# The last token group of two feed-forward layers: products of 128 rows cut into two of 64 rows, summed apart and joined by VectorE

## The chip, the cores and the metric

The kernel runs on one core of a Trainium2 chip. The metric is the device time of one execution in microseconds (us). The engines are called as the profile calls them: PE is TensorE's matmul, PEld its load of stationary operands, DVE is VectorE, ACT is ScalarE, POOL is GpSimd and SP is SyncE, which issues the DMAs here. A *product* is one matmul instruction with the load that belongs to it.

## The reference

A windowed attention gives 1536 tokens of 512 values; two feed-forward layers of 512 -> 2048 -> 512 follow. The changed code is the end of the second one.

```python
def _moe2_ref(x, w_in, w_out) -> np.ndarray:
    h = x @ w_in
    relu6 = np.clip(h + 3.0, 0.0, 6.0)
    g = h * relu6 / 6.0
    return (g @ w_out).astype(np.float32)

def reference(**kwargs):
    ...
    attn_out = _attn_ref(**attn_kwargs)
    B, H, S, D = attn_out.shape
    x = np.ascontiguousarray(attn_out.transpose(0, 2, 1, 3)).reshape(B * S, H * D)
    x = _moe_ref(x=x, **moe_kwargs)
    return _moe2_ref(x=x, **moe2_kwargs)
```

## The kernel before

The 1536 tokens are three groups of 512 (`GB`), and the 2048 hidden values sixteen chunks of 128 (`NCH`), whose weights pass through the core in phases of 6, 5 and 5 chunks per layer (`PHASES`). Each operand of the layers stands as a high and a low float32r part (`xsh` and `xsl`, `gh` and `gl`, two weight tiles each), and each mathematical product is three products on the chip: low by high, high by low, high by high, in that order of all three over the list it is given (`matmul3`, L209; its instruction is L214, which all layer products share in the profile).

`item` (L277) does one chunk for one group: twelve products of 128 rows by 512 columns make `h` in one PSUM bank (four parts of the 512 inputs, `KC`, by three), ACT and DVE make `gh` and `gl` from it (`split_g`, L184: ACT's relu at L203, DVE's product at L204, ACT's cast to `gh` at L205, DVE's subtraction to `gl` at L206), and twelve more products add to four sums `acc`, one per 128 tokens. In the second layer `gh` and `gl` are the stationary operand of those.

The last group of the last phase is `last_items` (L323). It makes the five `h` (named `hz`) and their `g` first, calls `check_step` between them (which at its end puts one small transposition `pf`, L666, on PE), and then takes the 128 tokens `m` one after the other: fifteen products into one sum `accz`, the three of a chunk together, one DVE instruction that adds a sixth of it to `part` (L355), one DMA of the result. The last 128 tokens go as two halves of 256 columns, to end on a short piece. PSUM banks rotate: `h_bank` (L98) goes round four banks by its count `n_h`, `acc_tags` names the four banks of the sums.

The order of the instructions on each engine is not that of the code alone: the context is opened with `schedule_with_timeline_sim=True` (L871), so a planner with costs of its own sets it, and PE, ACT and DVE each work through their own list in that order. Products of the group before (`acc`) therefore stand between those of the last one.

Of the kernel before, what the change touches and what calls it, by code (L numbers as in the profile page):

```python
# [7 lines left out]
F32 = mybir.dt.float32  # L8
# [4 lines left out]
ALU = mybir.AluOpType  # L13
# [3 lines left out]
P = 128  # L17
# [4 lines left out]
KC = DM // P  # L22
# [4 lines left out]
GT, GB = 256, 512  # L27
# [27 lines left out]
class Layers:  # L55
# [153 lines left out]
    def matmul3(self, out, pairs, start, stop, **kw):  # L209
# [3 lines left out]
        def one(z, a, b):  # L213
            return self.nc.tensor.matmul(  # L214
                out, lhsT=a, rhs=b, start=start and z == 0, stop=stop and z == len(seq) - 1, **kw
            )

        return [lambda z=z, ab=ab: one(z, *ab) for z, ab in enumerate(seq)]

    def first_items(self):  # L220


        n = PHASES[0][0] // 2
        runs = [(g, 0, EARLY_PAIRS) for g in range(EARLY)] + [(EARLY, 0, n)]
        runs += [(g, EARLY_PAIRS, n) for g in range(EARLY)] + [(g, 0, n) for g in range(EARLY + 1, T // GT)]
        return [(g, s, s == a, s == b - 1, a > 0) for g, a, b in runs for s in range(a, b)]
# [96 lines left out]
    def last_items(self, ph, G, spare_step):  # L323


        nc, part = self.nc, self.part[G]
        if self.hint:
            self.tc.mark_branch_hint_location("redo", engines=list(mybir.ALL_ENGINES))
        g, W = [], []
        for s in range(PHASES[1][ph]):  # L330
            W.append(self.W[NCH + sum(PHASES[1][:ph]) + s])
            wih, wil = (t.rearrange("p (k c) -> p k c", k=KC) for t in W[s][0:2])
            h = self.h_bank(f"hz{s}")
            for call in self.matmul3(
                h, [((wih[:, c], wil[:, c]), (self.xsh[G][:, c, :], self.xsl[G][:, c, :])) for c in range(KC)], True, True
            ):
                call()
            wp, t = self.free.pop(0)
            where = [wp.tile([P, CW], F32R, tag=f"w{i}_{t}", name=f"g{i}_{s}") for i in range(2)]
            g.append(self.split_g(1, h, f"z{s}", where))  # L340
            for _ in range(4):
                spare_step()
        for m in range(4):
            acc = self.bank(self.acc_tags[m], f"accz{m}")
            t0 = G * GB + m * P
            ms = slice(m * P, (m + 1) * P)
            for cs in (slice(0, 512),) if m < 3 else (slice(0, 256), slice(256, 512)):
                if cs.start:
                    acc = self.h_bank("accz4")
                for s, (gh, gl) in enumerate(g):  # L350
                    pair = ((gh[:, ms], gl[:, ms]), (W[s][2][:, cs], W[s][3][:, cs]))
                    for call in self.matmul3(acc[:, cs], [pair], s == 0, s == len(g) - 1, skip_group_check=True):
                        call()
                pm = part[:, m, cs]
                nc.vector.scalar_tensor_tensor(  # L355
                    out=pm, in0=acc[:, cs], scalar=1.0 / 6.0, in1=pm, op0=ALU.mult, op1=ALU.add
                )
                nc.sync.dma_start(out=self.out[t0:t0 + P, cs], in_=pm)
# [516 lines left out]
```

## Time and profile before

| | us |
|---|---|
| median of three runs | 630.69 (630.36 to 631.89) |
| the profiled execution, whole | 630.09 |
| its span, first to last instruction | 628.3 |
| PE busy in the span | 613.8 (98%) |
| DVE, ACT, POOL busy | 448.8, 375.3, 132.0 |
| first product of the last group (`hz`) | at 591.44 |
| last DVE instruction of the span's results | at 624.60, 0.42 long |

A busy PE says only that some product is in it: the record of a product is longer than the distance to the next one, since products overlap at their ends. What a product costs is read from start to start, and where a line of the timeline merges several, from the merged duration less that of one record. Times in the timeline count from the start of the span.

### The profile page before, as it was taken

The numbers are of one execution on the slowest core, as the hardware profiler recorded it, in microseconds if no ns is written. First come the engines' busy times: TensorE is split into PE (matmuls) and PEld (weight loads), VectorE is DVE, ScalarE is ACT, GpSimd is POOL, SyncE is SP. The second block draws the span as 40 slices with busy tenths as digits, with TensorE's granted clock in tenths as the row PEclk, the third lists the DMA queues.
The fourth block names the chain that finished last, engine by engine and source line by source line (L and its number), as shares of the span: only waits on it lengthen the run. The fifth ranks groups of instructions, "written<-read, shape, count | busy, mean of one in ns | idle before, by whom it ended". The sixth has DMA issues, their size and how long they took to land.

```text
span 628.3 us, 9717 instructions
## 1 busy us (share of the span) xinstructions
PE 613.8 (98%) x3495; PEld 514.8 (82%) x3496; DVE 448.8 (71%) x945; ACT 375.3 (60%) x796; POOL 132.0 (21%) x168
## 2 busy tenths in 40 slices
PE   8898999999999999999999999999999999999997
PEld 4587878899999888877788888888888888888886
DVE  7995687635799999999998996224999633424262
ACT  6986888774778887776788852425455742222130
POOL 3474353430132233533301410000100000000000
PEclk9998999999999999999999999999999999999999
DMA  8763312101144343333401143001457620001011
GB/s 278 272 196 106 106 39 69 35 14 68 68 133 137 96 139 119 123 107 117 140 34 57 45 135 101 1 1 33 142 191 233 207 67 1 1 0 68 1 67 69
DMA packets 26804, 59.91 MB, mean 95 GB/s; under 512 B 2688, under 2 KB 9344, under 8 KB 26752
## 3 DMA queue, kind: packets, MB, share of 16 engines
q1 hardware_dynamic: 26752, 59.26, 28.8%
q8 instruction: 28, 0.46, 0.3%
q14 instruction: 24, 0.20, 0.1%
HBM read 56.10 MB, written 3.15 MB: 94 GB/s over the span
## 4 chain that ended last, share of the span: by engine, by line
PE 74%; DVE 18%; ACT 4%; issue 2%; POOL 1%; DMA 0%; SPq 0%; POOLq 0%; ACTq 0%; DVEq 0%
PE acc L214 25%; PE h L214 24%; PE accf L214 8%; PE hf L214 6%; ACT pm L548 3%; PE ptp L571 2%; DVE wa L146 2%; PE accz L214 2%; PE hz L214 2%; PE px L589 2%; DVE wa L147 2%; DVE w L152 2%; PE s L537 2%; DVE t L200 1%; DVE t L199 1%
## 5 line engine op out<-in xcount | busy, mean ns | idle before, releaser
L214 PE MATMUL h<-xsh,w 128*128 128x512 f32 x584 | 154.7, 390 | 0.4 <-DVE t L200 0.4
L214 PEld LDWEIGHTS h<-xsh,w 128*128 128x128 f32 x584 | 109.1, 188 | 24.1 <-DVE t L200 1.8
L140 POOL TENSOR_SCALAR wa<-wa 128x512 f32<-128x512 f32 x52 | 67.4, 1300 | 242.7 <-ACT wa L137 242.7
L214 PE MATMUL acc<-w,gh 128*128 128x512 f32 x344 | 105.9, 389 | 0.0
L214 PE MATMUL h<-xsl,w 128*128 128x512 f32 x292 | 80.8, 389 | 0.0
L206 DVE TENSOR_TENSOR gl<-t,gh 128x512 fp32r<-128x512 f32 x73 | 51.3, 703 | 40.5 <-ACT gh L205 40.4
L214 PE MATMUL acc<-gh,w 128*128 128x512 f32 x240 | 77.7, 391 | 1.2 <-ACT gh L205 1.0
L214 PEld LDWEIGHTS acc<-w,gh 128*128 128x128 f32 x344 | 64.6, 188 | 13.5
L203 ACT ACTIVATE t<-h,three 128x512 f32<-128x512 f32 x43 | 29.5, 687 | 75.2 <-PE h L214 75.0
L204 DVE SCALAR_TENSOR_TENSOR t<-t,h 128x512 f32<-128x512 f32 x43 | 29.4, 684 | 61.4 <-ACT t L203 61.3
L432 POOL TENSOR_SCALAR pm<-pm,rs 128x256 f32<-128x256 f32 (+1 forms) x96 | 56.6, 607 | 67.5 <-DVE rs L430 31.8
L205 ACT CAST gh<-t 128x512 fp32r<-128x512 f32 x73 | 45.2, 619 | 41.4 <-PE acc L214 23.3
L214 PE MATMUL acc<-w,gl 128*128 128x512 f32 x172 | 66.9, 389 | 0.0
L214 PEld LDWEIGHTS h<-xsl,w 128*128 128x128 f32 x292 | 54.7, 188 | 11.4
L214 PE MATMUL accf<-ghf,w 128*128 128x256 f32 x288 | 58.7, 293 | 0.5 <-ACT ghf L205 0.5
L214 PEld LDWEIGHTS acc<-gh,w 128*128 128x128 f32 x240 | 44.8, 188 | 11.6 <-ACT gh L205 1.9
L548 ACT ACTIVATE pm<-pm,nm 128x256 f32<-128x256 f32 (+1 forms) x96 | 46.2, 483 | 5.6 <-DVE nm L543 5.3
L214 PEld LDWEIGHTS accf<-ghf,w 128*128 128x128 f32 x288 | 47.8, 196 | 0.9 <-ACT ghf L205 0.8
L214 PE MATMUL hf<-xsh,w 128*128 128x256 f32 x288 | 47.1, 289 | 0.0
L214 PE MATMUL acc<-gl,w 128*128 128x512 f32 x120 | 46.7, 389 | 0.0
L151 ACT CAST w<-wa 128x512 fp32r<-128x512 f32 x56 | 34.4, 615 | 17.3 <-DVE wa L147 9.6
L214 PE MATMUL accf<-glf,w 128*128 128x256 f32 x144 | 41.5, 288 | 1.5 <-DVE glf L206 1.5
(122 smaller groups left out, 1060.1 us busy)
## 6 DMA issues: line engine op xcount, KB each, us to landing
raw<-in_w2i SPq DMA_DIRECT2D x16, 512.0 KB, 3.3
raw<-in_w2o SPq DMA_DIRECT2D x16, 512.0 KB, 3.3
raw<-in_w1i SPq DMA_DIRECT2D x14, 512.0 KB, 3.8
raw<-in_w1o SPq DMA_DIRECT2D x12, 512.0 KB, 3.3
V<-in_v SPq DMA_DIRECT2D x12, 256.0 KB, 3.3
range<-in_w1i SPq DMA_DIRECT2D x6, 512.0 KB, 3.7
range<-in_w1o SPq DMA_DIRECT2D x6, 512.0 KB, 4.4
chk<-in_q SPq DMA_DIRECT2D x12, 256.0 KB, 2.7
```

The costliest lines, as they stand in the source:

```text
L140: nc.gpsimd.tensor_scalar(out=a, in0=a, scalar1=W_HI, scalar2=W_LO, op0=ALU.min, op1=ALU.max)
L146: nc.vector.scalar_tensor_tensor(out=ai, in0=hi, scalar=-2 ** 30, in1=ai, op0=ALU.bitwise_and, op1=ALU.bitwise_or)
L147: nc.vector.scalar_tensor_tensor(out=ai, in0=lo, scalar=29, in1=ai, op0=ALU.logical_shift_right, op1=ALU.bitwise_or)
L151: nc.scalar.copy(wh, a)
L152: nc.vector.tensor_tensor(out=wl, in0=a, in1=r32(wh), op=ALU.subtract)
L203: nc.scalar.activation(t1, hf, AF.Relu, bias=self.three[:, 0:1])
L204: nc.vector.scalar_tensor_tensor(out=t3, in0=t1, scalar=6.0, in1=hf, op0=ALU.min, op1=ALU.mult)
L205: nc.scalar.copy(gh, t3)
L206: nc.vector.tensor_tensor(out=gl, in0=t3, in1=r32(gh), op=ALU.subtract)
L214: return self.nc.tensor.matmul(out, lhsT=a, rhs=b, start=start and z == 0, stop=stop and z == len(seq) - 1, **kw)
L432: nc.gpsimd.tensor_scalar(out=t, in0=t, scalar1=rs[:, j:j + 1], scalar2=0.0, op0=ALU.mult, op1=ALU.add)
L548: nc.scalar.activation(pmz, pmz, AF.Exp, bias=nm[:, z:z + 1], scale=-1.0, accum_out=sm[:, z:z + 1])
```

## The change

`last_items` alone is changed. Each product of 128 rows in it, but for those of the last 128 tokens, becomes two of 64 rows, rows 0 to 63 and rows 64 to 127 of both operands, which lie in the upper and the lower half of the array. Each half has a sum of its own in a bank of its own (`matmul3_rows`). For `h`, ACT copies the first sum to an SBUF tile `hsz` and DVE adds the second to it there, and `split_g` works on that tile. For the tokens, DVE adds both sums to `part`, one after the other, so that a pair of banks serves `m` = 0 and 2, the other `m` = 1. Two things come with it: the fifteen products of a sum are now ordered low by high over all five chunks first, then high by low, then high by high; and the planner makes a new order of the whole group.

```diff
+    def matmul3_rows(self, outs, pairs):
+
+        seq = [(a[x], b[y]) for x, y in ((1, 0), (0, 1), (0, 0)) for a, b in pairs]
+        for z, (a, b) in enumerate(seq):
+            for r, out in enumerate(outs):
+                rows = slice(r * P // 2, (r + 1) * P // 2)
+                self.nc.tensor.matmul(out, lhsT=a[rows], rhs=b[rows], start=z == 0, stop=z == len(seq) - 1)
...
-            h = self.h_bank(f"hz{s}")
-            for call in self.matmul3(
-                h, [((wih[:, c], wil[:, c]), (self.xsh[G][:, c, :], self.xsl[G][:, c, :])) for c in range(KC)], True, True
-            ):
-                call()
+            hs = [self.h_bank(f"hz{s}_{r}") for r in range(2)]
+            self.matmul3_rows(
+                hs, [((wih[:, c], wil[:, c]), (self.xsh[G][:, c, :], self.xsl[G][:, c, :])) for c in range(KC)]
+            )
+            h = self.tp.tile([P, 512], F32, tag="t", name=f"hsz{s}")
+            nc.scalar.copy(h, hs[0])
+            nc.vector.tensor_tensor(out=h, in0=hs[1], in1=h, op=ALU.add)
...
-        for m in range(4):
-            acc = self.bank(self.acc_tags[m], f"accz{m}")
+        for m in range(3):
+            accs = [self.bank(self.acc_tags[2 * (m % 2) + r], f"accz{m}_{r}") for r in range(2)]
+            ms = slice(m * P, (m + 1) * P)
+            self.matmul3_rows(accs, [((gh[:, ms], gl[:, ms]), W[s][2:4]) for s, (gh, gl) in enumerate(g)])
+            pm = part[:, m, :]
+            for acc in accs:
+                nc.vector.scalar_tensor_tensor(
+                    out=pm, in0=acc, scalar=1.0 / 6.0, in1=pm, op0=ALU.mult, op1=ALU.add
+                )
+            t0 = G * GB + m * P
+            nc.sync.dma_start(out=self.out[t0:t0 + P, :], in_=pm)
+        for m in (3,):
+            acc = self.bank(self.acc_tags[2], f"accz{m}")
...
-            for cs in (slice(0, 512),) if m < 3 else (slice(0, 256), slice(256, 512)):
+            for cs in (slice(0, 256), slice(256, 512)):
```

Up to the first `hz` all engines have the same list as before. From there on the order differs. Three places of it follow; `hz_0`, `accz_0` are sums of the upper half, `hz_1`, `accz_1` of the lower, and L226 (after) is the new product line, L214 that of whole products in both.

The first is PE's list at the start of the group, where the `acc` products of the group before come in between. Before:

```order
L214 MATMUL hz_92_6161<-xsh_77,w_27_4878 128x512 x4
L214 MATMUL hz_92_6161<-xsl_80,w_27_4877 128x512 x4
L214 MATMUL hz_92_6161<-xsh_77,w_27_4877 128x512
L214 MATMUL acc_5985<-w_30_5157,gl_6090 128x512
L214 MATMUL acc_5985<-w_30_5158,gh_6089 128x512
```

After:

```order
L226 MATMUL hz_1_93_6162<-xsh_77,w_27_4878 128x512
L226 MATMUL hz_0_92_6161<-xsh_77,w_27_4878 128x512
L226 MATMUL hz_1_93_6162<-xsh_77,w_27_4878 128x512
L226 MATMUL hz_0_92_6161<-xsl_80,w_27_4877 128x512
L214 MATMUL acc_5985<-w_30_5157,gl_6090 128x512
L214 MATMUL acc_5985<-w_30_5158,gh_6089 128x512
```

Half products stand in turn, upper and lower, and whole products follow them directly; here they cut in after an upper one whose lower one comes twelve whole products later.

The second is PE's list at the fourth and fifth chunk. Before:

```order
L666 MATMUL pf_6264<-ident,m_6257 1x128
L214 MATMUL hz_96_6275<-xsh_77,w_30_5156 128x512 x4
L214 MATMUL hz_96_6275<-xsl_80,w_30_5155 128x512 x4
L214 MATMUL hz_96_6275<-xsh_77,w_30_5155 128x512 x4
L214 MATMUL accz_6317<-w_27_4879,g_0_6175 128x512
L214 MATMUL hz_97_6296<-xsh_77,w_31_5258 128x512 x4
```

After:

```order
L226 MATMUL hz_0_99_6323<-xsh_77,w_30_5155 128x512 x4
L226 MATMUL accz_0_6397<-w_27_4879,g_0_6191 128x512
L226 MATMUL accz_1_6398<-w_27_4879,g_0_6191 128x512
L226 MATMUL accz_0_6397<-w_28_4969,g_1_6240 128x512
L226 MATMUL accz_1_6398<-w_28_4969,g_1_6240 128x512
L226 MATMUL accz_0_6432<-w_27_4879,g_0_6191 128x512
L226 MATMUL accz_1_6433<-w_27_4879,g_0_6191 128x512
L226 MATMUL accz_0_6432<-w_28_4969,g_1_6240 128x512
L226 MATMUL accz_1_6433<-w_28_4969,g_1_6240 128x512
L226 MATMUL hz_1_100_6324<-xsh_77,w_30_5156 128x512 x4
L226 MATMUL hz_1_100_6324<-xsl_80,w_30_5155 128x512 x4
L226 MATMUL hz_1_100_6324<-xsh_77,w_30_5155 128x512 x4
```

The fourth chunk's twelve upper products (the last four are the first row) all stand ahead of its twelve lower ones, with four pairs of `accz` between.

The third is where the last chunk's `g` is first used (`g_4`; of the two tiles with that name, the one with the higher last number is `gl`). PE before:

```order
L214 MATMUL accz_6353<-w_30_5157,g_3_6289 128x512
L214 MATMUL accz_6317<-w_31_5259,g_4_6310 128x512
L214 MATMUL accz_6317<-w_31_5260,g_4_6309 128x512
L214 MATMUL accz_6317<-w_31_5259,g_4_6310 128x512
L214 MATMUL accz_6335<-w_31_5259,g_4_6310 128x512
```

PE after:

```order
L226 MATMUL accz_0_6397<-w_30_5157,g_3_6353 128x512
L226 MATMUL accz_1_6398<-w_30_5157,g_3_6353 128x512
L226 MATMUL accz_0_6432<-w_30_5157,g_3_6353 128x512
L226 MATMUL accz_1_6433<-w_30_5157,g_3_6353 128x512
L214 MATMUL accz_103_6520<-w_30_5157,g_3_6353 128x256
L214 MATMUL accz_103_6520<-w_30_5158,g_3_6352 128x256
L214 MATMUL accz_103_6520<-w_30_5157,g_3_6352 128x256
L226 MATMUL accz_0_6397<-w_31_5259,g_4_6390 128x512
L226 MATMUL accz_1_6398<-w_31_5259,g_4_6390 128x512
L226 MATMUL accz_0_6397<-w_27_4880,g_0_6190 128x512
```

DVE's list that makes those `g`, before:

```order
L204 SCALAR_TENSOR_TENSOR t3z_6291<-t1z_6290,hz_96_6275 128x512
L206 TENSOR_TENSOR g_3_6289<-t3z_6291,g_3_6288 128x512
L204 SCALAR_TENSOR_TENSOR t3z_6312<-t1z_6311,hz_97_6296 128x512
L206 TENSOR_TENSOR g_4_6310<-t3z_6312,g_4_6309 128x512
L355 SCALAR_TENSOR_TENSOR part_92<-accz_6317,part_92 128x512
```

DVE after:

```order
L347 TENSOR_TENSOR hsz_6349<-hz_1_100_6324,hsz_6349 128x512
L204 SCALAR_TENSOR_TENSOR t3z_6355<-t1z_6354,hsz_6349 128x512
L206 TENSOR_TENSOR g_3_6353<-t3z_6355,g_3_6352 128x512
L347 TENSOR_TENSOR hsz_6386<-hz_1_102_6361,hsz_6386 128x512
L204 SCALAR_TENSOR_TENSOR t3z_6392<-t1z_6391,hsz_6386 128x512
L206 TENSOR_TENSOR g_4_6390<-t3z_6392,g_4_6389 128x512
```

Before, 33 whole products stand on PE between the last `hz` and the first use of `g_4`; after, eight half products and twelve whole ones of 256 columns do. On DVE one instruction more stands in each chunk's chain, behind the subtraction of the chunk before.

## Rows read from the trace of the kernel before

**Rows 1.** The page: span, busy time, granted clock in 40 slices (tenths).

```profile
span 628.3 us, 9717 instructions
PE 613.8 (98%) x3495; PEld 514.8 (82%) x3496; DVE 448.8 (71%) x945; ACT 375.3 (60%) x796; POOL 132.0 (21%) x168
...
PEclk9998999999999999999999999999999999999999
```

**Rows 2.** The chain that ended last: start us, us, what, instructions.

```profile
611.00 13.58 PE accz L214 x74
```

**Rows 3.** Timeline, PE and PEld, last group: start us, us, instructions merged.

```profile
591.44 1.07 PE L214 MATMUL hz<-xsh,w 128*128 128x512 f32 x4
...
608.11 1.07 PE L214 MATMUL hz<-xsh,w 128*128 128x512 f32 x4
608.80 0.87 PEld L214 LDWEIGHTS hz<-xsl,w 128*128 128x128 f32 x4
609.02 1.07 PE L214 MATMUL hz<-xsl,w 128*128 128x512 f32 x4
...
610.83 13.72 PE L214 MATMUL accz<-w,g 128*128 128x512 f32 x74
```

**Rows 4.** Timeline of PE, warm-up products of bf16, whole array.

```profile
10.22 0.81 PE L683 MATMUL warm<-zeros 128*128 128x512 bf16 x3
```

**Rows 5.** Timeline of PE in the attention, one pair of half products each.

```profile
121.23 0.29 PE L214 MATMUL accf<-ghf,w 128*128 128x256 f32 x1
121.44 0.49 PE L537 MATMUL s<-kT,qT 64*128 64x256 f32 x2
121.77 0.38 PE L537 MATMUL s<-kT,qT 64*128 64x256 f32 x2
121.98 0.38 PE L537 MATMUL s<-kT,qT 64*128 64x256 f32 x2
122.20 0.38 PE L537 MATMUL s<-kT,qT 64*128 64x256 f32 x2
```

**Rows 6.** Timeline of PE, from halves (of columns) back to whole products.

```profile
143.93 0.50 PE L589 MATMUL px<-pT,V 128*64 128x128 f32 x6
144.15 0.28 PE L589 MATMUL px<-pT,V 128*64 128x128 f32 x2
144.36 0.74 PE L214 MATMUL hf<-xsh,w 128*128 128x256 f32 x4
144.93 0.64 PE L214 MATMUL hf<-xsl,w 128*128 128x256 f32 x4
```

**Rows 7.** Timeline of ACT and DVE, the last chunk's `g`.

```profile
611.09 0.69 ACT L203 ACTIVATE t1z<-hz,three 128x512 f32<-128x512 f32 x1 [0.88 <-PE hz L214]
611.81 0.69 DVE L204 SCALAR_TENSOR_TENSOR t3z<-t1z,hz 128x512 f32<-128x512 f32 x1 [0.88 <-ACT t1z L203]
612.54 0.62 ACT L205 CAST g<-t3z 128x512 fp32r<-128x512 f32 x1 [0.76 <-DVE t3z L204]
613.19 0.69 DVE L206 TENSOR_TENSOR g<-t3z,g 128x512 fp32r<-128x512 f32 x1 [0.69 <-ACT g L205]
```

**Rows 8.** Timeline, the end of the span.

```profile
624.60 0.42 DVE L355 SCALAR_TENSOR_TENSOR part<-accz,part 128x256 f32<-128x256 f32 x1 [1.37 <-PE accz L214]
```

**Rows 9.** PE's two longest waits near the start, in brackets.

```profile
22.30 0.44 PE L589 MATMUL px<-pT,V 128*64 128x128 f32 x4 [1.05 <-ACT pT L573]
...
51.18 0.38 PE L214 MATMUL accf<-glf,w 128*128 128x256 f32 x1 [1.46 <-DVE glf L206]
```

**Rows 10.** Stretches: length, PE, PEld, DVE, ACT, POOL busy, granted clock, DMA.

```profile
51.00:52.00 1.00, 0.82 (x5) 0.82 (x6) 1.00 (x3) 1.00 (x5) 0.00 (x0) 0.75 0.80 188
52.00:53.00 1.00, 1.00 (x6) 1.00 (x6) 1.00 (x4) 0.97 (x4) 0.00 (x0) 0.50 0.24 90
...
54.00:55.00 1.00, 1.00 (x7) 1.00 (x6) 0.69 (x1) 0.25 (x1) 1.00 (x2) 0.55 0.00 0
...
591.00:625.00 34.00, 33.56 (x163) 28.13 (x161) 14.44 (x25) 7.86 (x12) 0.00 (x0) 1.00 0.16 59
```

## The prediction, made before the changed kernel ran

> **What bounds the kernel now.** I read the page first: PE is busy in 613.8 of 628.3 us [rows 1], so the kernel is as long as its products. Then the chain that ended last, whose last long piece is the `accz` products [rows 2]: what is lost or won on PE in the last group moves the end. Then the timeline of that group. It starts at 591.44, PE never waits in it, and the 74 `accz` products go through in one piece from 610.83 [rows 3]. The granted clock is 1.00 (2.4 GHz) from 591 to 625 [rows 10].
>
> The pitch from product to product is what the change is about. Four products start at 608.11 and the next four at 609.02 [rows 3]: 0.91 / 4 = 0.227 us for 512 columns of float32r. Products of 256 columns stand 0.12 apart (four in 0.64, less one record of 0.29, by three [rows 5, 6]). 512 columns in bf16, over the whole array too, take (0.81 - 0.38) / 2 = 0.215, with 0.38 for one record [rows 4]. So a float32r product pays about 0.012 more than that, whether it is long or short. That is all that halving can win.
>
> **What half products cost, by the attention.** There the trace has products in two halves of 64 rows. Each line "x2" at L537 is one pair, one for each half, and both lie inside one record's length, so the halves do run side by side. Pairs start at 121.77, 121.98 and 122.20: 0.215 a pair [rows 5]. They are float32, not float32r: whether a float32r pair goes at 0.215 or 0.227 the trace doesn't show. From below I bound it by 0.215 (the pair's row), from above by 0.227 + 0.012 = 0.239 (both halves pay the extra one after the other). I take **0.227**: rows 3 and 4 differ in the type alone and not in the geometry, and each half still has as many float32r products to swap in as the whole array had.
>
> The attention also shows what a change of geometry costs. From whole to halves: the last whole product starts at 121.23, the first pair at 121.44, 0.21 where 0.12 would be the pitch; and the first pair takes 0.32 to the second where 0.215 is the pitch [rows 5]. That is 0.09 + 0.11 = 0.20. Back from halves (here of columns): the pitch of pairs is (0.50 - 0.28) / 2 = 0.11, the last pair starts at 144.15 and the first whole product at 144.36, 0.10 too much; its four take 0.57 to 144.93 where 4 x 0.12 is usual [rows 6]. Again 0.19. I take **0.20 a switch**.
>
> The Trainium skill has a rule against this change ("TensorEngine Tiling (Array Packing)", Key Properties): a change of tiling mode drains TensorE. The rows agree on the drain, the first 0.09 of each switch, but show a second part of the same size after it that the rule doesn't name. By the rule alone the twelve switches below would cost 1.1 instead of 2.4 us.
>
> **The path, part by part.** Nothing changes before 591.44, since the lists are the same up to there. I call the time in which the array takes one half product, or one in each half, a slot.
>
> *Slots.* Before, the changed work is 60 `hz` and 45 `accz` products: 105 times 0.227. Afterwards it is 210 half products; paired throughout they would be 105 slots again. But PE works its list in order. Counted through the new order: the first three chunks' 72 need 37 slots, since one pair is torn by twelve `acc` products. The next 60 (fourth and fifth chunk and twelve `accz`) need 42, not 30, since twelve upper ones in a row and then twelve lower ones can't run side by side. The next 4 need 2, the last 74 need 37. Together 118, **13 more: 13 x 0.227 = 2.95 us**. The 24 `acc` products and the 30 of 256 columns stay as they are.
>
> *Switches.* The list goes from whole to half products and back twelve times: at the start, around two blocks of `acc` (four), around `pf` (two), and five from the 256-column products: **12 x 0.20 = 2.4 us**. Before there is none.
>
> *A wait for the last `g`.* The new ACT copy and DVE add lengthen the chain from `h` to `gl`. Before, ACT starts 0.48 after the last `hz` product started (610.61 by the pitch, 611.09), and relu, product, cast and subtraction end 2.79 after that, at 613.88 [rows 7]; 33 whole products cover it. In the new list I reach the last `hz` product at 591.44 + 76 slots (17.2) + 24 `acc` (5.45) + 7 switches (1.4) = 615.5. The same way, the fourth chunk's last product starts 12 slots earlier, at 612.8; its add (0.69, bounded by the L204 row, which also reads a sum and an SBUF tile [rows 7]) runs from 613.3 to 614.0, and its subtraction ends at 616.8. The fifth chunk's copy ends at 616.5 and its add would be ready for DVE then, but stands behind that subtraction in DVE's list. So it ends at 617.5, and `gl` is there at 617.55 + 2.79 = 620.35. PE arrives earlier: from 615.5, three slots (0.68), a switch, nine products of 256 columns (1.08), a switch, two slots (0.45), a switch, three products (0.36), a switch: 618.9. It **waits 1.45 us**, everything of PE is queued behind it, and as `gl` is the stationary operand, its load is exposed once more, 0.1 by the first pair of rows 5.
>
> Other additions cost nothing: ACT and DVE are busy 7.9 and 14.4 of the 34 us from 591 to 625 [rows 10], so the copies and adds of the first chunks lie under the next chunks' products; the sums' banks come free before they are needed (`m` = 2 starts 11 slots, 2.5 us, after `m` = 0 ended, against two DVE instructions of 0.69). If that cover failed, each would cost its 0.7.
>
> *The tail.* The last DVE instruction of 256 columns takes 0.42 [rows 8]. The last two sums now end 0.36 apart, so the last one waits for the first: 0.42 + 0.03 - 0.36 = 0.09.
>
> **Sum:** 2.95 + 2.4 + 1.45 + 0.1 + 0.09 = 7.0, less 0.1 for the switch to `pf`, whose single column needs no load: **+6.9 us**. On the profiled execution's own 630.09 that is 637.0; that execution lies 0.6 under the median of the runs, 630.69, so the forecast is **637.6 us**. A nanosecond more or less on a slot is worth 0.10 us: 64 slots lie ahead of the fourth chunk's last product, which sets the chain to the wait, and 37 behind the wait.
>
> **Rivals.**
>
> 1. The swap is hidden: a pair takes 0.215. For it: the pair rows, and the bf16 row. Against: both are other types. The sum falls by 101 x 0.012 = 1.2: **636.4**. The Trainium skill ("TensorE: Matmul & The Clock Gate", Part 3) says that a load overlaps a running matmul only when their row groups differ, from which halving would gain. This trace doesn't bear that out for whole products: four loads, 0.87 us from 608.80, lie under the products from 608.11 [rows 3], and a load of 0.19 fits in a pitch of 0.227 only so. I give it the chance that rows 4 and 5 give.
>
> 2. Both halves pay their swap in turn, 0.239 a pair, 1.2 more: **638.8**. Nothing in the trace shows it.
>
> 3. The clock falls at the wait. After the 1.46 us wait at 51.18 [rows 9] the granted clock was 0.50 (1.2 GHz) until about 54.9 [rows 10], though PE was at work again; a wait of 1.05 at 22.3 [rows 9] left it at 0.9 or more in its slice, the second, where the fourth, with 51.18 in it, shows 8 [rows 1]. Mine is 1.45, between the two and nearer to the one that fell; but PE is busy right up to it. Price: 3.4 us at half speed, 1.7 us: **639.3**.
>
> 4. The change doesn't do what it says: float32r halves don't run side by side. Then 210 half products take 210 x 0.227, 92 slots more, 20.9 us, less 1.2 as the wait all but goes: **657**. Against it are the pairs of rows 5, two banks, two halves, as here.
>
> 5. The other side, not slower: a half product takes less than a whole one. The place is the slot. The point from which it decides: 0.227 - 6.9 / 101 = 0.159 for no loss at all, 0.177 for less than 0.3% (1.9 us, about what a measurement of this kernel can tell from no change). At 0.159 it is **631**. For it: only that the pair's record, 0.38, is a little shorter than the whole one's 0.39. Against: the pairs' pitch of 0.215, which is the pitch of 512 columns in bf16 too.
>
> **How the numbers follow.** Forecast 40%, rival 1 24%, rival 2 10%, rival 3 12%, rival 4 9%, rival 5 5%. Switches at the drain alone (0.1) with rival 1 give 635.4, the wait being longer by half of what they save; rival 2 and the clock together give 640.5. The range 635.4 to 640.6 holds the first four cases, 86%, and leaves out 4 and 5. All but rival 5 are slower by over 0.3%, 95%; of its 5%, 3 lie within 0.3% and 2 below.
>
> **What the profile of the changed kernel would show.** Pairs of L226 0.227 apart, upper and lower a few ns from each other: slot and concurrency right; at 0.215 rival 1, single ones at 0.227 throughout rival 4. First pairs after a whole product late by 0.09 and long by 0.11: the switch. Twelve upper `hz` of the fourth chunk in series over 2.7 us: the 13 slots. PE idle 1.2 to 1.7 us at about 619 to 620.4, released by DVE's L206: the wait; a granted clock under 1.00 after it is rival 3. The forecast is wrong above all if the switch of this type costs other than the float32 rows say, twelve times, or if the copy and add are slow enough to move the wait.

## The result, and the profile after

The changed kernel takes 638.89 us (median of 4 runs, 638.02 to 639.66) against 630.87 for the kernel before (4 runs, 630.36 to 631.89): a ratio of 1.0125, 95% interval 1.0106 to 1.0143. That is 8.0 us slower. In a second comparison, described below, it took 638.35 against 631.17, 7.2 us slower (1.011, 1.007 to 1.015). The forecast was 6.9 slower, 637.6 us.

The page of the first profiled execution, which took 639.66 us, answers [rows 1]:

```profile
span 637.9 us, 9948 instructions
...
PE 621.0 (97%) x3601; PEld 517.5 (81%) x3601; DVE 454.2 (71%) x953; ACT 378.0 (59%) x801; POOL 131.7 (21%) x168
...
PEclk9998999999999999999999999999999999999999
```

PE has 106 records more and is 7.2 us longer busy, in a span that is 9.6 longer. (105 products are new; the trace of before lacks the record of one, which has its load among the 3496 of PEld.) I cut that span by two starts of products on PE. The last `h` product before the group starts at 592.34 (591.21 before), the last product of all at 633.48 (624.28 before). So the time up to the group grew by 1.13 us, the group itself from 33.07 to 41.14, by 8.07, and what follows the last product from 4.02 to 4.38, by 0.36. The first of these isn't the change's doing: up to there the lists are the same, and in the profiles below that start lies anywhere between 591.2 and 593.1, while runs of the kernel before spread over 629.2 to 633.3 us.

The timeline of PE at the start of the group (columns as in [rows 3]; 64x512 is a half product) shows what the pieces cost:

```profile
591.66 1.07 PE L214 MATMUL h<-xsh,w 128*128 128x512 f32 x4
592.66 1.20 PE L226 MATMUL hz<-xsh,w 64*128 64x512 f32 x8
593.70 0.38 PE L226 MATMUL hz<-xsl,w 64*128 64x512 f32 x1
594.01 0.50 PE L214 MATMUL acc<-w,gl 128*128 128x512 f32 x1
594.35 0.63 PE L214 MATMUL acc<-w,gh 128*128 128x512 f32 x2
```

Four whole products from 591.66 would be through at 592.57; the first pair starts at 592.66, so 0.09 is lost. Eight half products end 1.20 after that. Taken singly the two of a pair start 3 ns apart, and the pairs 0.335, then 0.23 apart (0.227 in longer rows of pairs): the halves do lie side by side, the first pair takes 0.11 too long, and a pair takes what a whole product takes. Back to whole products it is the same: 0.31 to the next start at 594.01, where 0.227 is the pitch, and 0.34 to the one after.

The end of the group, PE again, with its wait in brackets, answers [rows 3] and [rows 7]:

```profile
617.07 1.33 PE L214 MATMUL accz<-w,g 128*128 128x256 f32 x9
618.33 0.73 PE L226 MATMUL accz<-w,g 64*128 64x512 f32 x4
619.00 0.62 PE L214 MATMUL accz<-w,g 128*128 128x256 f32 x3
621.14 10.29 PE L226 MATMUL accz<-w,g 64*128 64x512 f32 x74 [1.52 <-DVE g L206]
631.35 2.41 PE L214 MATMUL accz<-w,g 128*128 128x256 f32 x18
```

PE stands still for 1.52 us until DVE's last subtraction. And the 74 half products behind the wait take 10.21 us to the next start, where 37 pairs of 0.227, a first load and a switch need 8.6. The windows show why (the columns of [rows 10]):

```profile
621.00:622.00 1.00, 0.86 (x4) 0.78 (x6) 0.08 (x1) 0.00 (x0) 0.00 (x0) 0.60 0.03 8
622.00:623.00 1.00, 1.00 (x8) 0.73 (x8) 0.00 (x0) 0.00 (x0) 0.00 (x0) 0.50 0.00 0
...
624.00:625.00 1.00, 1.00 (x10) 0.80 (x8) 0.00 (x0) 0.00 (x0) 0.00 (x0) 0.69 0.00 0
625.00:626.00 1.00, 1.00 (x12) 0.87 (x10) 0.45 (x1) 0.00 (x0) 0.00 (x0) 1.00 0.00 0
```

The granted clock was 0.50 (1.2 GHz) from 621.2 to 624.6, right behind the wait. Eight products lie in a microsecond at 0.50, twelve in one later: 10.21 less 8.6, some 1.6 us, are lost. The page's row of slices, a mean over 16 us each, doesn't show it at all.

The chain of waits (start, length, what) tells why the last `g` is late, and answers [rows 7]:

```profile
614.01 0.70 DVE hsz L347
...
616.28 0.63 ACT g L205
616.97 0.57 issue
617.54 0.69 DVE hsz L347
...
619.74 0.63 ACT g L205
620.39 0.70 DVE g L206
```

"issue" at 616.97 is DVE at the fourth chunk's subtraction (616.93, 0.69 long); the fifth chunk's add stands behind it in DVE's list and starts when it is through. This is the step that the prediction named.

### The profile page after: what moved, and what is told of

It reads as the page before. It is cut to its first block, busy times and chain, and to the rows that moved or that the text cites. A ratio compares the mean times of both kernels' runs of the same rounds, so it can differ in the third digit from the quotient of the medians.

```text
span 637.9 us, 9948 instructions
## 1 busy us (share of the span) xinstructions
PE 621.0 (97%) x3601; PEld 517.5 (81%) x3601; DVE 454.2 (71%) x953; ACT 378.0 (59%) x801; POOL 131.7 (21%) x168
## 4 chain that ended last, share of the span: by engine, by line
PE 62%; DVE 22%; ACT 6%; DMA 5%; issue 3%; POOL 1%; ACTq 0%; SPq 0%; POOLq 0%; DVEq 0%
PE acc L214 19%; PE h L214 18%; PE accf L214 8%; PE hf L214 6%; DVE wa L146 3%; DVE w L152 3%; ACT pm L569 3%; DVE wa L147 2%; PE ptp L592 2%; PE hz L226 2%; DMA chk<-in_k 2%; PE px L610 2%; DMA chk<-in_q 2%; DVE gl L206 2%; PE accz L226 2%
## 5 line engine op out<-in xcount | busy, mean ns | idle before, releaser
L214 PE MATMUL h<-xsh,w 128*128 128x512 f32 x584 | 154.7, 390 | 0.3 <-DVE t L200 0.3
L214 PEld LDWEIGHTS h<-xsh,w 128*128 128x128 f32 x584 | 109.1, 188 | 24.2 <-DVE t L200 1.9
L214 PE MATMUL acc<-w,gh 128*128 128x512 f32 x344 | 106.0, 389 | 0.0
L214 PE MATMUL h<-xsl,w 128*128 128x512 f32 x292 | 80.8, 389 | 0.0
L214 PE MATMUL acc<-gh,w 128*128 128x512 f32 x240 | 77.7, 391 | 1.2 <-ACT gh L205 1.0
L214 PEld LDWEIGHTS acc<-w,gh 128*128 128x128 f32 x344 | 64.6, 188 | 13.3
L214 PE MATMUL acc<-w,gl 128*128 128x512 f32 x172 | 67.4, 392 | 0.6 <-DVE gl L206 0.6
L214 PEld LDWEIGHTS h<-xsl,w 128*128 128x128 f32 x292 | 54.7, 188 | 11.4
L214 PE MATMUL accf<-ghf,w 128*128 128x256 f32 x288 | 58.6, 292 | 0.4 <-ACT ghf L205 0.4
L214 PEld LDWEIGHTS acc<-gh,w 128*128 128x128 f32 x240 | 44.8, 188 | 11.6 <-ACT gh L205 1.9
L214 PEld LDWEIGHTS accf<-ghf,w 128*128 128x128 f32 x288 | 47.8, 197 | 0.8 <-ACT ghf L205 0.7
L214 PE MATMUL hf<-xsh,w 128*128 128x256 f32 x288 | 47.1, 289 | 0.0
L214 PE MATMUL acc<-gl,w 128*128 128x512 f32 x120 | 46.7, 389 | 0.0
L137 ACT ACTIVATE wa<-raw 128x512 f32<-128x512 f32 x52 | 34.9, 675 | 14.3 <-DVE w L152 6.9
```

The source lines that it names most:

```text
L137: first = nc.scalar.activation(a, raw.bitcast(F32)[:, :, 1], AF.Abs)
L214: return self.nc.tensor.matmul(out, lhsT=a, rhs=b, start=start and z == 0, stop=stop and z == len(seq) - 1, **kw)
```

## The experiments

In what follows "group" is the distance that was 33.07 before and 41.14 in the first profile of the change, and "tail" what follows the last product. Both are of the profiled execution; "median" is of all runs. Experiments were made against 631.46 us (19 runs of the kernel before) in the first set, 631.52 (11) in the second, 629.65 (one) for the microbenchmark and 631.17 (6) in the last three.

### Is it the two sums or the halves?

`e1_two_sums_whole` keeps all that is new but for the halves: two sums per result, the copy, the adds, and the new order of operands, with whole products that go to the two sums in turn.

```diff
-            for r, out in enumerate(outs):
-                rows = slice(r * P // 2, (r + 1) * P // 2)
-                self.nc.tensor.matmul(out, lhsT=a[rows], rhs=b[rows], start=z == 0, stop=z == len(seq) - 1)
+            self.nc.tensor.matmul(outs[z % 2], lhsT=a, rhs=b, start=z < 2, stop=z >= len(seq) - 2)
```

> Two sums for every product sum as in the change, the same low parts first, the same copy and add, but whole products of 128 rows that go to the two sums in turn; no halves. Theory (the loss is the geometry: half products in series, switches between whole and half products, and the wait that the longer chain makes behind them): 105 products as before, no switch, the chain covered by whole products, so 0 to +0.3 us on 630.87. Rival (the loss is in joining two sums, by copy, add and a second DVE instruction per sum): +5 us or more, as in the change.

Measured: 631.23 (12 runs), ratio 1.0003 (0.9987 to 1.0018), group 33.15. Joining two sums with ACT and DVE costs nothing as long as whole products, in the order that the planner gives them, cover it. What the change costs comes from the half products, directly or by what the planner does with them.

### One part of the change at a time

`e2_tokens_only` makes `h` as before, and halves only the products of the tokens:

```diff
-            hs = [self.h_bank(f"hz{s}_{r}") for r in range(2)]
...
+            h = self.h_bank(f"hz{s}")
+            for call in self.matmul3(
+                h, [((wih[:, c], wil[:, c]), (self.xsh[G][:, c, :], self.xsl[G][:, c, :])) for c in range(KC)], True, True
+            ):
+                call()
```

> Halves in the products for the tokens alone, h by whole products into one sum, without copy and add. Theory: 90 half products in 48 slots where 45 would do (3 x 0.227 = 0.7), 8 switches (1.6), no wait, since the chain to g is as before: +2.3, about 633.2. If half products side by side cost more than whole ones the sum is larger by 48 times the difference.

Measured: 634.80 (6 runs), ratio 1.0056 (1.0038 to 1.0075), 3.3 us over before. The group is 34.91, 1.84 longer, with eight switches and no wait; the tail is 5.61, 1.6 longer. `e3_h_only` is the other half of the change:

```diff
-        for m in range(3):
-            accs = [self.bank(self.acc_tags[2 * (m % 2) + r], f"accz{m}_{r}") for r in range(2)]
...
+        for m in range(4):
+            acc = self.bank(self.acc_tags[m], f"accz{m}")
...
```

> Halves in the products of h alone, with copy and add; the tokens by whole products, the three of a chunk together. Theory: 120 half products in 73 slots where 60 would do (13 x 0.227 = 2.95), 10 switches (2.0), no wait, since the order by chunks needs the last g later: +5.0, about 635.8. Rival (the chain with copy and add costs by itself): PE waits for DVE's L206 in the trace, and the time is above 636.5.

Measured: 637.28 (4 runs), ratio 1.0092 (1.0067 to 1.0117), 5.8 over before. The group is 38.16, 5.1 longer, the tail 5.22, 1.2 longer. In both the group grew by what was expected within half a microsecond, and the median by 0.8 to 1.0 more than expected; the tails of the two profiles are longer by more than that. The tail of `e3` has the very code of the kernel before. The tail is taken up in the section after the experiments.

### Does the order of the operands bring the wait?

`e4_chunk_order` keeps the halves and takes the three products of a chunk together again, as the kernel before does.

```diff
...
-            self.matmul3_rows(accs, [((gh[:, ms], gl[:, ms]), W[s][2:4]) for s, (gh, gl) in enumerate(g)])
+            for s, (gh, gl) in enumerate(g):
+                self.matmul3_rows(accs, [((gh[:, ms], gl[:, ms]), W[s][2:4])], s == 0, s == len(g) - 1)
```

> The change with the three products of a chunk together again in the sums of the tokens. Theory: the last g is needed later, so the wait falls from 1.5 to about 0.3 us and the granted clock stays at 1.00 behind it; the planner's order has 122 slots (17 x 0.227 = 3.85 more than before) and 10 switches (2.0): +6.0, about 637, some 2 us under the change although it has four slots more. Rival (the wait and the clock cost nothing, the slots are all): 0.5 us over the change.

Measured: 635.58 (4 runs), ratio 1.0071 (1.0045 to 1.0097), 4.1 over before, with a group of 38.07, 5.0 longer. PE doesn't wait in it and the clock stays up:

```profile
615.38 6.37 PE L226 MATMUL accz<-w,g 64*128 64x512 f32 x49
621.68 2.04 PE L214 MATMUL accz<-w,g 128*128 128x256 f32 x15
623.65 4.02 PE L226 MATMUL accz<-w,g 64*128 64x512 f32 x30
```

The wait is gone, so the order "low by high over all five chunks first" is needed for it: that order asks for the last `g` in its fifth product. It isn't enough for it: `e1` has the same order, and `e2` has it for the tokens, and PE waits in neither. The size was wrong by 1 us, in a term that the prediction shares: I had counted the half products that can't run side by side in the new list as 17 extra slots. The trace has 93 pairs (starts less than about 0.12 us apart) and 24 single ones: 117, only 12 more than 105. In `e2` it is 44 pairs and 2 single ones, 46 where I had counted 48; 1 x 0.227 and eight switches of 0.20 make 1.83, and its group grew by 1.84. Why is seen below, where the 13 slots of the prediction are gone through.

### A fixed order: whole products, halves, more switches

The next three set PE's order of the tokens' products by hand (`ordered`), the same in all of them: for each chunk `m` = 0 and 1, then the 24 products of 256 columns that don't need the last `g`, then the last chunk and `m` = 2. `e6_pinned_whole` has whole products into two sums (the lines with a minus), `e5_pinned_pairs` half products (those with a plus).

```diff
-            c = count["n"] = count.get("n", -1) + 1
-            self.ordered(lambda: self.nc.tensor.matmul(
-                outs[c % 2], lhsT=a, rhs=b, start=c < 2, stop=c >= total - 2
-            ))
+            for r, out in enumerate(outs):
+                rows = slice(r * P // 2, (r + 1) * P // 2)
+                self.ordered(lambda: self.nc.tensor.matmul(
+                    out, lhsT=a[rows], rhs=b[rows], start=first and z == 0, stop=last and z == len(seq) - 1
+                ))
```

> Whole products into two sums with copy and add, in an order fixed by hand: all h, then chunks 0 to 3 for m = 0 and 1, the last 128 tokens' chunks 0 to 3, then the last chunk, m = 2 and the rest. The control of the next run. Theory: 105 whole products, no switch, no wait: 0 to +0.3 us on 630.87.

> The same order and the same sums as the control, but half products, upper and lower in turn, so that nearly all stand in pairs: 106 slots for 210 halves, 10 switches, no wait. Theory: 1 x 0.227 + 10 x 0.20 = +2.2 us over the control, about 633.1. Rival 1 (a pair hides the swap, 0.215): +1.0. Rival 2 (a pair pays both swaps, 0.239): +3.5. Not under before in any case.

Measured: 634.10 for the whole ones (6 runs, ratio 1.0034, 1.0021 to 1.0047) and 637.82 for the halves (4 runs, 1.0106, 1.0091 to 1.0122). The control missed: it should have been the kernel before, and is 2.6 slower. The timelines of PE, `e6` first and then `e5`:

```profile
606.06 0.47 PE L226 MATMUL hz<-xsh,w 128*128 128x512 f32 x1
606.70 0.98 PE L226 MATMUL hz<-xsh,w 128*128 128x512 f32 x3 [0.17 <-ACT hsz L348]
...
623.33 3.47 PE L226 MATMUL accz<-w,g 128*128 128x512 f32 x14 [0.79 <-DVE part L382]
```

```profile
606.72 0.50 PE L226 MATMUL hz<-xsh,w 64*128 64x512 f32 x1
608.39 1.19 PE L226 MATMUL hz<-xsh,w 64*128 64x512 f32 x7 [1.18 <-ACT hsz L348]
...
625.09 3.70 PE L226 MATMUL accz<-w,g 64*128 64x512 f32 x29 [0.30 <-DVE part L382]
```

My own order makes PE wait for banks: for the copy that empties an `h` bank, and for the adds of `m` = 0 before `m` = 2. I hadn't counted these; they lengthen the group of `e6` to 35.03, 2.0 over before, and its tail is 6.13, 2.1 over. Halves against whole is then 3.13 in the group (38.16 less 35.03) where 2.2 was expected. The waits for banks differ between the two, 1.0 longer behind `pf` (1.18 against 0.17) and 0.5 shorter ahead of `m` = 2 (0.30 against 0.79), which is about half of what is missing. The other half is slots: the trace of `e5` has 102 pairs and 6 single half products, 108 instead of 106, 0.45 more, and two of the single ones (606.72 and 624.29) stand right at the waits. So this pair says that halves don't win here, and not what a switch costs. For that `e9_more_switches` takes the order of `e5` and spreads the 24 products of 256 columns into eight blocks of three (the edit is shown against `e5`):

```diff
-                if (s, m) == (4, 0):
-                    for h in range(2):
-                        for z in range(4):
-                            last_of(z, h)
...
+                    if m < 2:
+                        last_of(s, m)
```

> The pinned pairs with the last 128 tokens' whole products put between the pairs in eight places instead of one: the same 106 slots, 24 switches instead of 10. Theory (0.20 a switch): 14 x 0.20 = +2.8 us over the pinned pairs, about 635.9. Drain alone (0.09): +1.3.

Measured: 640.22 (4 runs, ratio 1.0138, 1.0118 to 1.0157), 2.4 over `e5` in the medians. The bank waits are the same to 0.01 us, the tails too (5.80 both), and the group is 41.02, 2.86 more than in `e5`: 14 more switches at **0.204 us** each. A stretch of it:

```profile
616.77 0.62 PE L214 MATMUL late<-w,g 128*128 128x256 f32 x3
617.32 0.96 PE L226 MATMUL accz<-w,g 64*128 64x512 f32 x6
618.22 0.62 PE L214 MATMUL late<-w,g 128*128 128x256 f32 x3
```

From one block of three whole products to the next it is 1.45 us, for three times 0.12 and three pairs of 0.227, which is 1.04. The 0.41 above that are two switches. The drain alone, 0.09, would have given 1.3 for the 14.

### The pitch by itself

`e8_pitch` is one run with rows of products of zeros in the warm-up, ten of each kind: pairs of halves, whole ones, upper halves alone, whole ones; first bf16, then float32r.

```diff
+        for t, n in ((zeros, "b"), (zr, "r")):
+            for kind in ("pairs", "whole", "upper", "whole"):
+                for _ in range(10):
+                    for r in range(2 if kind == "pairs" else 1):
+                        rows = slice(0, P) if kind == "whole" else slice(r * P // 2, (r + 1) * P // 2)
...
+                            two[r], lhsT=t[rows, 0:P], rhs=t[rows], start=True, stop=True
```

> The kernel before with products of zeros put into its start, ten each of: pairs of halves, whole, upper halves alone, whole; first in bf16, then in float32r, all with 512 columns. It is read for pitches and switches alone, its time means nothing. Theory: whole 0.215 in bf16 and 0.227 in float32r; pairs the same as whole in each type, so the extra 0.012 belongs to the type; upper halves alone as long as a whole product each; a switch 0.09 + 0.11 in both types. Rival (halves hide the swap): float32r pairs at 0.215.

Measured (start, length with the last record whole, count; the clock full throughout), bf16 pairs, upper halves and whole ones, then float32r pairs, whole ones, upper halves:

```profile
8.32 2.33 PE L695 MATMUL warm<-zeros 64*128 64x512 bf16 x20
12.85 2.33 PE L695 MATMUL warm<-zeros 64*128 64x512 bf16 x10
15.11 2.33 PE L695 MATMUL warm<-zeros 128*128 128x512 bf16 x10
...
17.37 2.56 PE L695 MATMUL warm<-zr 64*128 64x512 f32 x20
19.87 2.59 PE L695 MATMUL warm<-zr 128*128 128x512 f32 x10
22.39 2.56 PE L695 MATMUL warm<-zr 64*128 64x512 f32 x10
```

In each type the three lines are the same length to 0.03 us in ten: the geometry makes no difference to the pitch. In bf16 it is 0.216, with 0.223 to 0.227 after the first; in float32r 0.227 where it has settled, with 0.335 after the first and up to 0.236 in the five or six that follow; the ten whole ones don't settle before their end, which makes their line 2.59. So 2.33 against 2.56 is 0.11 for the first product, 0.1 for the 0.011 more of each of nine, and the rest is settling. The 0.012 of the prediction is a matter of the type, and a half product pays it like a whole one.

### The clock after the wait

`e7_fill` puts dummy products of 128 rows, whose sum nobody reads, into the order ahead of the first use of the last `g`; in the trace it is eight, one after the other, 1.82 us.

```diff
+        fill = self.h_bank("fill")
+        for _ in range(8):
+            nc.tensor.matmul(fill, lhsT=g[3][0][:, 0:P], rhs=self.xsh[G][:, 0, :], start=True, stop=True)
```

> The change with five whole products of no use (into a bank of their own) before the last g is needed, where PE waits. Theory (the clock falls because PE stands still there): the granted clock stays at 1.00 after the place and the pairs behind it keep 0.227; the wait shrinks to 0.3; the planner's order has two slots more: +7.4, about 638.3, a little under the change although PE does 1.1 us more. Rival (the clock falls whatever PE did, at its time of the run): 0.50 shows at about 621 again, and the time is 639.5 to 640.

Measured: 637.53 (4 runs, ratio 1.0089, 1.0073 to 1.0104), 1.4 under the 638.89 of the change, with no wait and the clock at 1.00; the group is 39.77. I first read this as the clock's price, given back. But that compared two profiles of two sets. So the change itself ran once more, beside fills of two and of five products on the same chip (the edit is the one above, with 2 and 5 for the 8).

> The changed kernel itself, once more, on the chip of the two fill runs below. If the fall of the granted clock after the wait for the last g belongs to the change and not to one execution, its profile shows PE standing still for about 1.5 us, 0.50 for some 3.4 us behind that, and a time about 8.0 us over the kernel before. If the fall of the first profile was an accident, no fall and 6.4 over it.

> Two dummy products of 0.227 us, whose sum nobody reads, stand ahead of the first use of the last g, so that PE stands still for about 1.5 - 0.45 = 1.05 us there. The arrival of g sets the end of that, so the products cost nothing. If the clock stays up with a stop of this length (as it did behind the 1.05 us at 22.3 us in the kernel before), the time is 1.6 us under the changed kernel, group 39.5 us; if any stop brings the fall, the same as the changed kernel, 41.1.

> Five dummy products in the same place: 1.14 us of work, a stop of about 0.4 us left. With the clock up, again 1.6 us under the changed kernel; the group takes the 39.5 us of the run with two. If it comes out lower still, the fill does something else than keep PE at work.

Measured: 638.35 for the change (4 runs, 637.46 to 639.74), 638.73 with two products, 638.34 with five, all against 631.17: ratios of 1.011, 1.0116 and 1.0102, each 0.004 wide to either side. PE's waits and the granted clock behind them in the three profiles, the change first:

```profile
620.81 5.51 PE L226 MATMUL accz<-w,g 64*128 64x512 f32 x46 [1.52 <-DVE g L206]
...
621.00:622.00 1.00, 1.00 (x10) 0.84 (x10) 0.00 (x0) 0.00 (x0) 0.00 (x0) 1.00 0.02 8
622.00:623.00 1.00, 1.00 (x13) 0.87 (x12) 0.00 (x0) 0.00 (x0) 0.00 (x0) 1.00 0.00 0
```

```profile
620.81 5.53 PE L226 MATMUL accz<-w,g 64*128 64x512 f32 x46 [1.06 <-DVE g L206]
```

```profile
621.24 5.06 PE L226 MATMUL accz<-w,g 64*128 64x512 f32 x42 [0.39 <-DVE g L206]
```

The same wait of 1.52 us stands in the second profile of the change, and this time the clock stayed at 1.00 behind it. The groups are 39.53, 39.56 and 39.56 long: what PE does before the last `g` comes is free, as the arrival of `g` sets the end of the wait, and even the eight products of `e7` cost only what they are longer than the wait (39.53 - 1.59 + 1.82 = 39.76, measured 39.77). The fall of the clock came in one of two profiles of the change, and in none of the three fills. So the fill shows that the wait hides 1.5 us of work; that it saved the clock it does not show.

## Why the prediction was right, and where it was off

The sign and the mechanism came out as forecast, and the time lies 1.3 us from the forecast's 637.6. That it lies so near is partly luck: the slots cost less than forecast and the tail more, and in some executions the clock fell besides. The second profile of the change (638.82 us, 8.73 over the profiled execution of before, 630.09) lets the terms be compared, since no clock fell in its group:

| | predicted | measured, us |
|---|---|---|
| slots | 13 x 0.227 = 2.95 | 11 x 0.227 = 2.50 |
| switches, with `pf` | 2.4 - 0.1 | ten at 0.200 and 0.28 around `pf`: 2.28 |
| wait for the last `g` with its load | 1.45 + 0.1 | 1.59 |
| settling and rest | none | 0.10 |
| **group** | **6.8** | **6.47** |
| tail | 0.09 | 1.46 (first profile 0.36) |
| before the group | 0 | 0.80 (first profile 1.13) |

**The slot** is 0.227 as taken, from [rows 3, 4] by the argument that the type alone differs; the microbenchmark shows just that. Rivals 1 (0.215), 2 (0.239), 4 (not side by side) and 5 (shorter) fall with it. The pair rows were no bound for it: their products have 256 columns, in float32, and at 0.215 they take nearly twice the 0.12 that 256 columns of float32r take [rows 5, 6]. That this is also the pitch of 512 columns in bf16 says nothing of float32r halves, though rival 1, and what stood against rival 5, leaned on it. The rows show that halves lie side by side, and what a switch costs.

**The number of slots** was off by two. I had counted by "PE works its list in order", as the section on the kernel before says it too, and that isn't quite what the records show. The fourth chunk's twelve upper products in the second profile of the change:

```profile
607.49 1.20 PE L226 MATMUL hz<-xsh,w 64*128 64x512 f32 x4
608.53 1.08 PE L226 MATMUL hz<-xsl,w 64*128 64x512 f32 x4
609.45 0.62 PE L226 MATMUL hz<-xsh,w 64*128 64x512 f32 x2
609.69 0.50 PE L226 MATMUL accz<-w,g 64*128 64x512 f32 x1
609.91 0.39 PE L226 MATMUL hz<-xsh,w 64*128 64x512 f32 x1
610.03 0.40 PE L226 MATMUL accz<-w,g 64*128 64x512 f32 x1
610.14 0.39 PE L226 MATMUL hz<-xsh,w 64*128 64x512 f32 x1
610.27 0.71 PE L226 MATMUL accz<-w,g 64*128 64x512 f32 x4
```

They go through in series as forecast, 0.23 each. But products of the lower half, which stand behind all twelve in the list, start at 609.69 and 610.03, before the last two of them. So the two halves run past each other by a little at the end of a series, and again at 612.58, where the fifth chunk's upper products start beside the fourth's last lower ones. The 60 products took 9.06 us (607.49 to 616.75, less a first load and a drain), 40 slots where I had counted 42. The same step made the expectation of `e4` too high.

**The switch** is right, and the best tested term: 0.20 from the float32 rows of the attention [rows 5, 6], 0.204 by `e9`. The 0.1 that the prediction took off for `pf` is right in size and not in its reason: `pf` does have a load, 0.08 long in both traces, and its two switches together cost 0.28 more than `pf` cost before. The Trainium skill ("TensorEngine Tiling (Array Packing)", Key Properties) names only the drain. For float32r this case doesn't agree (0.09 of 0.20); for bf16 it does: in the microbenchmark the last whole product is 0.31 from the first pair instead of 0.216 (and the last upper half, at 14.80, as far from the first whole one at 15.11), and that is nearly all.

**The wait** is right to 0.05 us: `e4` shows that it doesn't come without the new order of operands, and the chain of waits that it ends with the fifth chunk's add behind the fourth's subtraction.

**What else lies there costs nothing**, as forecast: `e1` shows it for the joining as long as whole products cover it.

**The clock.** The fall that the first profile shows is rival 3, priced at 1.7 and measured at 1.6. I gave it 12%. With the same wait it came in one of two profiles, so 12% looks low, though two profiles give no chance. The mean granted clock of the eight timed executions of the change is 0.994 or 0.995 in three, which took 638.91 to 639.74 us, and 0.996 to 1.0 in five, which took 637.46 to 638.87, with a median of 638.02. A fall of 3.4 us takes 0.003 off that mean, and every profile but that of `e2` has one before 58 us (that of `e8`, with its longer start, at 73). This fits a second fall in some of the executions; where it lay is seen in one only, and in `e1` both lie before 58 us. The mean alone doesn't place it behind this wait: the kernel before, which has no such wait, shows 0.994 or 0.995 in six of the 36 executions timed in the sets of 19, 11 and 6. I had judged the chance by the length of the stop, and that doesn't decide it: of the fourteen profiles, all with a stop of 1.35 to 1.55 us at that early place of [rows 9], twelve show the fall there and `e2` and `e9` none, and in `e1` and `e9` the clock fell at 29.9 and 30.5, with no stop over 0.52 in the 7 us before. What decides whether the clock falls behind this wait stays open.

**The tail** was the step that failed. I had taken only DVE into account, and its 0.09 isn't there: DVE's last instruction starts 0.32 after the last product's start before and in both profiles of the change. Two things come after it. First, the last two DMAs are now issued by SP one behind the other, and the first of the two takes 0.53 and 0.61 in the two profiles, where one took 0.33. Before, the first profile of the change, and the second:

```profile
625.05 0.33 SPq L358 DMA_DIRECT2D out_x<-part  x1
```

```profile
633.89 1.00 SPq L379 DMA_DIRECT2D out_x<-part  x2
```

```profile
631.96 1.09 SPq L379 DMA_DIRECT2D out_x<-part  x2
```

The last issue ends 0.78 after DVE's last start before, and 1.10 and 1.18 in the two profiles of the change: 0.3 to 0.4 of the tail. Second, the time from the last issue to its landing differs from profile to profile. These are the DMA issues in the last stretch of the kernel before (count, KB, us to landing), and of `e3`, whose end is the same code:

```profile
out_x<-part SPq DMA_DIRECT2D x1, 128.0 KB, 1.8
```

```profile
out_x<-part SPq DMA_DIRECT2D x1, 128.0 KB, 3.1
```

1.3 us between them is what the tail of `e3` has too much, and the two profiles of the change (1.9 and 2.5, medians of two) differ in the same way. That much of this isn't the change's is seen where the end is the same: `e8` ends as the kernel before does, and has a tail of 4.23 with a landing of 2.1. The change and its three fills end alike too, and in their five profiles the first of the two last issues takes 0.52 to 0.99, the landing 1.9 to 2.5 and the tail 4.2 to 5.5. What stays open is why seven of the ten variants have tails of 5.2 to 6.1, and with it up to 1 us of the 7.2 to 8.0.

**The range** was added up wrong at its lower end: 636.4 less 1.2 for the switches, and half of that longer in the wait, is 635.8 and not 635.4.

## What to carry to other kernels

Cutting a full product of 128 rows into two halves that run side by side won nothing here: a pair takes what the whole one takes, 0.227 us, and each change between whole and half products cost 0.20 us in float32r. Where products are halved for another reason, look in the new order for three things that cost more than the halving: series of one half only, switches, and a sum whose early products need the operand that is ready last. They are found by counting slots, switches and the chain through the compiled order, which gave the group's 6.5 us more here to 0.3 us; the end of the program, behind the last product, wants a look of its own.

## What the runs showed that I had not expected

- The exposed load after a switch belongs to the type: 0.335 instead of 0.227 after the first product in float32r, 0.223 to 0.227 instead of 0.216 in bf16. After it float32r half products need five or six more, at up to 0.236, to come back to 0.227, and whole ones ten or more.
- Products of the two halves don't keep the order of the list strictly: two lower ones started 0.22 and 0.11 us ahead of upper ones that stand before them. The Trainium skill ("TensorE: Matmul & The Clock Gate", Part 3, The mechanism) says that matmuls start and end in program order without reordering. The records here differ by these products, and shortened the series by two slots.
- The same stop of 1.52 us at the same place was followed by 3.4 us at 1.2 GHz in one execution and by none in another; stops of 1.06 and 1.18 us in the group of the variants were followed by none.
- A DMA of 128 KB at the end of the program, from the same code, took 1.8 us to land in the profile of the kernel before and 3.1 in that of `e3`, which alone is 0.2% of the time.
